# Decoding 64-bit weights: the guard for tiny values as a factor in ScalarE's operation

## The chip, the cores and the metric

The kernel runs on one core of one Trainium2 chip. The metric is the device time of one execution in microseconds (us). A core has five engines that run their own instruction streams in order and wait for one another through semaphores: TensorE (PE in the profile, with its weight loads shown apart as PEld), VectorE (DVE), ScalarE (ACT), GpSimd (POOL) and SyncE (SP), which here issues every DMA. The kernel before was timed in three runs: 1007.31, 1008.38 and 1008.51 us, the median 1008.38 us.

## The reference

Block-causal attention is followed by a gated product of matrices without a nonlinearity. The sizes are batch 8, 8 heads, 576 positions, 64 columns a head; blocks of 64.

```python
scores = scale * np.matmul(q, k.transpose(0, 1, 3, 2))
scores = np.where(block_i >= block_j, scores, -1e9)
attn = np.exp(scores - np.max(scores, axis=-1, keepdims=True))
attn = attn / (np.sum(attn, axis=-1, keepdims=True) + 1e-9)
x = np.matmul(attn, v)                  # laid out as 4608 tokens x 512
a, b = x @ w1, x @ w2                   # w1, w2: 512 x 1024
out = ((a * b @ w3) @ w_out)            # w3: 1024 x 1024, w_out: 1024 x 512
```

The inputs q, k and v are 32-bit floats. The four weight matrices arrive as 64-bit floats, because a 32-bit array was multiplied by a 64-bit scalar.

## The kernel before, in words

Two heads form a pair, and the 32 pairs (8 batches of 4) are worked through one after the other by `pair(n)`. For each pair, `shift_mask` finds row maxima (tiles `mx` on PE, reduced on DVE into `m`, transposed into `mt`, negated by ACT into `ms`, and written by a small DMA into a row of `qk`), `prep_qk` splits q and k into a rounded part and a remainder, `s_tile` makes scores `s` and their exponentials, `pv` or `pv_early` multiplies them with v into `x`, and `norm` and `finish_x` divide by the row sums and split the result into `xh` and `xl` (lines 320 to 333). `gen_moe` then multiplies a batch's four x tiles with w1 and w2 (line 381, tile `ab`) and with the product of w3 and w_out (line 397, tile `o`).

The first four pairs are the early stage. While their attention runs, `gen_w` brings in the weights. It loads 40 pieces of 128 partitions by 512 weights: eight of w_out (tile `wo`), then, in turn, two pieces of w3 (tile `w`) and one of w1 for each of eight steps, and at the end eight of w2. PE multiplies w3 by w_out in the early stage (line 358, 64 matmuls that the trace records as 128), so that only the product `wh`, `wl` is needed later. `load_w`, lines 122 to 143, turns each piece into 32-bit floats. It sees a 64-bit float as two 32-bit words, low and high. One ACT instruction takes the sign off the high word (line 135), one DVE instruction takes the maximum of that with 2 to the power -15 (line 136), one shifts it left by three bits and masks it (line 137), one puts the sign and the top exponent bit back (line 138), and one adds three bits of the low word (line 141). The five buffers `wraw` of the loaded words come free when line 141 has read them. Pieces of w1 and w2 also get a rounded copy by ACT (line 147) and a remainder by DVE (line 148).

The order of instructions on the engines in the early stage is written out in part by `EARLY_PLAN`, a string of steps; in it "C" advances the weight loader. A scheduler with priorities then places each instruction, so an edit in `load_w` can move others. In the main stage PE's order is that of `PLAN`. SP issues its DMAs in one queue, in order: a load that waits for a free buffer holds back those behind it.

Of the kernel before, what the change touches and what calls it, by code (L numbers as in the profile page):

```python
# [7 lines left out]
F32 = mybir.dt.float32  # L8
# [3 lines left out]
AF = mybir.ActivationFunctionType  # L12
ALU = mybir.AluOpType
# [45 lines left out]
def block_causal_attention__then__gated_mlp_kernel(ctx, tc, qkv, consts, ident_in, w1, w2, w3t, wout, out_t):  # L59
    nc = tc.nc  # L60
# [61 lines left out]
    def load_w(dst, src, k):  # L122

        t = tl["early"].tile([P, 1024], F32, tag="wraw", name="wraw", bufs=5)
        u = tl["early"].tile([P, 512], F32, tag="wbits", name="wbits", bufs=6)
        wide = t.bitcast(I32)
        nc.sync.dma_start(out=wide.rearrange("p (k w) -> p k w", k=k), in_=src)  # L130
        wide = wide.rearrange("p (c two) -> p c two", two=2)
        low, high = wide[:, :, 0], wide[:, :, 1]
        bits = u.bitcast(I32)
        V = nc.vector
        nc.scalar.activation(u, high.bitcast(F32), AF.Abs)
        V.tensor_scalar(out=u, in0=u, scalar1=2.0**-15, scalar2=None, op0=ALU.max)
        V.tensor_scalar(out=bits, in0=bits, scalar1=3, scalar2=0x3FFFFFF8, op0=ALU.logical_shift_left, op1=ALU.bitwise_and)
        V.scalar_tensor_tensor(out=bits, in0=high, scalar=-0x40000000, in1=bits, op0=ALU.bitwise_and, op1=ALU.bitwise_or)  # L138
        if dst is None:
            dst = u.unsqueeze(1)  # L140
        V.scalar_tensor_tensor(out=dst.bitcast(I32), in0=low.rearrange("p (k w) -> p k w", k=k), scalar=29,
                               in1=bits.rearrange("p (k w) -> p k w", k=k), op0=ALU.logical_shift_right, op1=ALU.bitwise_or)
        return u

    def load_split(dst_h, dst_l, src):
        val = load_w(None, src.unsqueeze(1), 1)
        nc.scalar.copy(dst_h, val)
        nc.vector.tensor_tensor(out=dst_l, in0=val, in1=dst_h, op=ALU.subtract)
# [187 lines left out]
    def gen_w(wp):  # L336
        wo = tl["wo"]
        for k in range(NF):
            load_w(wo[:, k : k + 1, :], wout[k * P : (k + 1) * P, :].unsqueeze(1), 1)
            yield  # L340
# [8 lines left out]
        for m in range(NF):  # L349
            t3 = wp.tile([P, NF, P], F32, tag="w3", name="w3", bufs=2)  # L350
            for k in range(0, NF, 4):
                src = w3t[k * P : (k + 4) * P, 2 * m * P : 2 * (m + 1) * P].rearrange("(k p) f -> p k f", p=P)
                load_w(t3[:, k : k + 4, :], src, 4)
                if k == 0:
                    yield
            acc = ps_m.tile([P, 512], F32, tag="psm", name=f"w{m}")
            for k in range(NF):
                nc.tensor.matmul(acc, t3[:, k, :], wo[:, k, :], start=(k == 0), stop=(k == NF - 1))  # L358
            pending.append((m, acc))
            if len(pending) > 1:  # L360
                evacuate()
            yield
            next(rows1)
            yield
# [172 lines left out]
```

## Time and profile before

| | |
|---|---|
| Time, median of three runs | 1008.38 us |
| Profiled execution, its own time | 1008.37 us |
| Span in its profile | 1006.6 us (so 1.77 us lie around it) |
| PE busy over the span | 961.6 us, 96% |
| DVE busy over the span | 718.8 us, 71% |
| ACT busy over the span | 547.9 us, 54% |
| Mean granted PE clock | 0.984 |
| DMA | 80.39 MB, mean 80 GB/s |

The shares are means over two very different stages. The early stage, to about 153 us, has DMA rates of some 250 GB/s at first and a full VectorE; in the main stage after it PE is full. A row of the timeline gives the start, the duration, engine, line and shapes, and in brackets how long the engine had been idle and who released it. PE's busy time is modelled, with matmuls overlapping, so a full PE is not one at its peak.

### The profile page before, as it was taken

To read this page: it belongs to the slowest core of one execution; us is meant where nothing else is said; L and a number is where in the kernel's file an instruction comes from. 1 tells how busy PE (TensorE), PEld (TensorE's weight loads), DVE (VectorE), ACT (ScalarE), POOL (GpSimd) and SP (SyncE) were. 2 spreads that over 40 slices of the span, in tenths; PEclk is the share of its full clock that TensorE was granted. 3 is DMA by queue.
4 is the path that set the end of the run, shared out by engine and by line. 5 is a ranking of instruction groups with operands and counts; after the bars stand their busy time and mean duration, and the time that the engine had idled before them with its cause. 6 is when DMAs were issued, how large, how long until landed. Compare 5 with 4: busy or idle time off the path is not lost.

```text
span 1006.6 us, 18165 instructions
## 1 busy us (share of the span) xinstructions
PE 961.6 (96%) x6594; PEld 886.1 (88%) x6624; DVE 718.8 (71%) x1356; ACT 547.9 (54%) x1433; POOL 521.1 (52%) x525
## 2 busy tenths in 40 slices
PE   4699958999999999999999999999999999999998
PEld 2354548999999999999999999999999999999998
DVE  7999997767777777777777767777777777774100
ACT  4655755555565655555555566555555655653211
POOL 0000006667665766666666657576666766573211
PEclk9799978999999999999999999999999999999999
DMA  8776522122212221221222222212212222110000
GB/s 247 240 257 195 170 82 61 55 80 61 85 57 78 61 74 38 70 73 56 78 61 85 61 74 61 84 32 67 73 58 76 61 85 61 37 24 25 1 25 24
DMA packets 36409, 80.39 MB, mean 80 GB/s; under 512 B 4384, under 2 KB 20896, under 8 KB 36320
## 3 DMA queue, kind: packets, MB, share of 16 engines
q1 hardware_dynamic: 36320, 79.23, 26.5%
q8 instruction: 52, 0.85, 0.4%
q14 instruction: 37, 0.30, 0.1%
HBM read 50.76 MB, written 9.44 MB: 60 GB/s over the span
## 4 chain that ended last, share of the span: by engine, by line
PE 60%; DVE 23%; ACT 9%; issue 6%; DMA 2%; DVEq 0%; ACTq 0%
PE ab L381 23%; PE o L397 20%; DVE pl L248 7%; PE s L230 6%; PE x L285 4%; PE mx L179 3%; DVE g L388 2%; ACT ph L246 2%; PE w L358 2%; ACT p L245 2%; DVE m L183 2%; DVE wbits L138 1%; DVE x L323 1%; DVE rb L322 1%; DVE qk L157 1%
## 5 line engine op out<-in xcount | busy, mean ns | idle before, releaser
L251 POOL TENSOR_TENSOR rsum<-rsum,p 128x448 f32<-128x448 f32 x224 | 178.3, 796 | 120.4 <-ACT p L245 113.6
L248 DVE TENSOR_TENSOR pl<-p,ph 128x448 fp32r<-128x448 f32 x168 | 150.9, 911 | 64.1 <-ACT ph L246 63.2
L389 ACT CAST gh<-g 128x288 fp32r<-128x288 f32 x128 | 55.5, 433 | 219.3 <-DVE g L388 219.3
L390 POOL TENSOR_TENSOR gl<-g,gh 128x288 fp32r<-128x288 f32 x128 | 108.3, 846 | 123.0 <-ACT gh L389 122.9
L230 PE MATMUL s<-qk 128*128 128x288 f32 (+4 forms) x768 | 160.7, 317 | 9.2 <-DMA qk<-ms 3.5
L381 PE MATMUL ab<-xh,w1h 128*128 128x288 f32 x512 | 152.0, 297 | 6.8 <-ACT xh L332 6.8
L381 PE MATMUL ab<-xh,w2h 128*128 128x288 f32 x512 | 154.1, 301 | 0.0
L397 PE MATMUL o<-gh,wh 128*128 128x288 f32 x512 | 153.4, 300 | 0.0
L381 PE MATMUL ab<-xh,w1l 128*128 128x288 f32 x512 | 151.6, 296 | 0.0
L381 PE MATMUL ab<-xl,w2h 128*128 128x288 f32 x512 | 151.5, 296 | 0.0
L381 PE MATMUL ab<-xl,w1h 128*128 128x288 f32 x512 | 151.5, 296 | 0.0
L381 PE MATMUL ab<-xh,w2l 128*128 128x288 f32 x512 | 151.4, 296 | 0.0
L397 PE MATMUL o<-gl,wh 128*128 128x288 f32 x512 | 150.8, 295 | 0.0
L397 PE MATMUL o<-gh,wl 128*128 128x288 f32 x512 | 150.8, 295 | 0.0
L207 POOL TENSOR_TENSOR qk<-raw,qk 64x1152 fp32r<-64x1152 f32 x54 | 144.3, 2672 | 2.0
L220 POOL TENSOR_TENSOR vs<-raw,vs 128x320 fp32r<-128x320 f32 x56 | 49.9, 891 | 174.2 <-ACT vs L157 174.2
L230 PEld LDWEIGHTS s<-qk 128*128 128x128 f32 (+1 forms) x768 | 116.9, 184 | 26.1 <-issue 6.1
L183 DVE TENSOR_REDUCE m<-mx 128x1 f32<-128x512 f32 (+6 forms) x320 | 128.6, 449 | 15.8 <-PE mx L179 13.2
L246 ACT ACTIVATE ph<-s 128x288 fp32r<-128x288 f32 x336 | 131.3, 392 | 0.0
L388 DVE TENSOR_TENSOR g<-ab,a 128x288 f32<-128x288 f32 x128 | 57.7, 451 | 74.4 <-PE ab L381 71.2
L245 ACT ACTIVATE p<-s 128x448 f32<-128x448 f32 x224 | 85.5, 382 | 45.8 <-PE s L230 44.2
L285 PE MATMUL x<-ph,vs 128*128 128x128 f32 x336 | 104.1, 319 | 0.0
(71 smaller groups left out, 2141.6 us busy)
## 6 DMA issues: line engine op xcount, KB each, us to landing
raw<-in_qkv SPq DMA_DIRECT2D x32, 896.0 KB
qk<-qk SPq DMA_DIRECT2D x64, 288.0 KB
out_t<-o SPq DMA_DIRECT2D x64, 144.0 KB
wraw<-in_w3t SPq DMA_DIRECT2D x16, 512.0 KB
wraw<-in_w SPq DMA_DIRECT2D x16, 512.0 KB
wraw<-in_wout SPq DMA_DIRECT2D x8, 512.0 KB
qk<-ms SPq DMA_DIRECT2D x64, 2.2 KB
cst<-in_consts SPq DMA_DIRECT2D x1, 288.0 KB
```

What stands on the lines that cost most here:

```text
L183: nc.vector.reduce_max(m[:, col : col + 1], sc, axis=AX.X)
L207: (nc.vector if n <= EARLY else nc.gpsimd).tensor_tensor(out=low, in0=rqk[o], in1=high, op=ALU.subtract)
L230: nc.tensor.matmul(t[ks, at : at + q1 - q0], qk[j][:, 2 + s, kr], qk[j][:, s, q0:q1], start=(s == 0), stop=(s == 1))
L245: nc.scalar.activation(p32, t[ks, at : at + w], AF.Exp, scale=SCALE)
L246: nc.scalar.activation(ph[ks, o : o + w], t[ks, at : at + w], AF.Exp, scale=SCALE)
L248: nc.vector.tensor_tensor(out=low, in0=p32, in1=ph[ks, o : o + w], op=ALU.subtract)
L251: nc.gpsimd.tensor_tensor(out=r, in0=r, in1=p32, op=ALU.add)
L285: nc.tensor.matmul(xps[:, to : to + w], v[:, c, :], pr[:, a : a + w], start=(u < 2 and s == 0), stop=(u in (0, len(PV) - 1) and s == len(p ...
L381: nc.tensor.matmul(t[:, 0:HALF], l[:, c, fs], r, start=(c == 0 and s == 0), stop=(c == NC - 1 and s == 2))
L388: nc.vector.tensor_tensor(out=g32, in0=acc[1][:, 0:HALF], in1=a32, op=ALU.mult)
L390: nc.gpsimd.tensor_tensor(out=gl[:, f, :], in0=g32, in1=gh[:, f, :], op=ALU.subtract)
L397: nc.tensor.matmul(t[:, 0:HALF], l[:, f, es], r[:, f, :], start=(f == 0 and s == 0), stop=(f == NF - 1 and s == 2))
```

## The change

The maximum on VectorE is taken out. ScalarE's operation, which takes the sign off, gets a factor of 2 to the power -112, so its output has an exponent field that is smaller by 112. After the shift by three bits this is the shift of the exponent by 896 that turns a 64-bit exponent into a 32-bit one, and what is too small comes out of ScalarE as a tiny number or zero. The two constants change with it: the mask lets the top exponent bit through, and from the high word only the sign is taken.

```diff
-        nc.scalar.activation(u, high.bitcast(F32), AF.Abs)
-        V.tensor_scalar(out=u, in0=u, scalar1=2.0**-15, scalar2=None, op0=ALU.max)
-        V.tensor_scalar(out=bits, in0=bits, scalar1=3, scalar2=0x3FFFFFF8, op0=ALU.logical_shift_left, op1=ALU.bitwise_and)
-        V.scalar_tensor_tensor(out=bits, in0=high, scalar=-0x40000000, in1=bits, op0=ALU.bitwise_and, op1=ALU.bitwise_or)
+        nc.scalar.activation(u, high.bitcast(F32), AF.Abs, scale=2.0**-112)
+        V.tensor_scalar(out=bits, in0=bits, scalar1=3, scalar2=0x7FFFFFF8, op0=ALU.logical_shift_left, op1=ALU.bitwise_and)
+        V.scalar_tensor_tensor(out=bits, in0=high, scalar=-0x80000000, in1=bits, op0=ALU.bitwise_and, op1=ALU.bitwise_or)
```

The line numbers after the change are one or two higher: shift and mask 138, sign 139, low bits 142, remainder 149, reduction 184, split of k and q 208, product with the reciprocal 324. The main stage's instructions keep their order on every engine. In the early stage the scheduler places them anew. Three places matter.

VectorE ahead of PE's first product of weights; `wo` is w_out's last piece and `w_313`, in the change `w_305`, the first half of the first tile of w3. Before:

```order
L138 SCALAR_TENSOR_TENSOR wbits<-wraw,wbits 128x512
L185 TENSOR_REDUCE m_213<-m_213 128x1
L136 TENSOR_SCALAR wbits<-wbits 128x512
L141 SCALAR_TENSOR_TENSOR wo<-wraw,wbits 128x512
L137 TENSOR_SCALAR wbits<-wbits 128x512
L136 TENSOR_SCALAR wbits<-wbits 128x512
L138 SCALAR_TENSOR_TENSOR wbits<-wraw,wbits 128x512
L137 TENSOR_SCALAR wbits<-wbits 128x512
L141 SCALAR_TENSOR_TENSOR wo<-wraw,wbits 128x512
L138 SCALAR_TENSOR_TENSOR wbits<-wraw,wbits 128x512
L136 TENSOR_SCALAR wbits<-wbits 128x512
L141 SCALAR_TENSOR_TENSOR w_313<-wraw,wbits 128x512
```

And in the change:

```order
L208 TENSOR_TENSOR qk_85<-raw_147,qk_85 64x1152
L184 TENSOR_REDUCE m_208<-mx_5_256 128x1 x2
L142 SCALAR_TENSOR_TENSOR wo<-wraw,wbits 128x512
L186 TENSOR_REDUCE m_208<-m_208 128x1
L138 TENSOR_SCALAR wbits<-wbits 128x512 x2
L139 SCALAR_TENSOR_TENSOR wbits<-wraw,wbits 128x512 x2
L142 SCALAR_TENSOR_TENSOR wo<-wraw,wbits 128x512
L142 SCALAR_TENSOR_TENSOR w_305<-wraw,wbits 128x512
```

The maxima are gone, and the last piece of w_out and the first of w3 now go through each step together, so the shift of w3's first piece stands four instructions ahead of the one that writes `w_305`. From VectorE's first instruction to that point ten instructions are left out and none is added.

VectorE at the end of the early stage, from the transposition of the last early row sums to the product that finishes x of the fourth pair. Before:

```order
L309 STREAM_TRANSPOSE tr_1_1107<-x_1_1034 64x576
L148 TENSOR_TENSOR w2l<-wbits,w2h 128x512
L138 SCALAR_TENSOR_TENSOR wbits<-wraw,wbits 128x512
L310 TENSOR_SCALAR rr_883<-tr_1_1107 64x18
L207 TENSOR_TENSOR qk_85<-raw_864,qk_85 64x1152
L141 SCALAR_TENSOR_TENSOR wbits<-wraw,wbits 128x512
L320 RECIPROCAL rr_883<-rr_883 128x18
L322 STREAM_TRANSPOSE rb_1112<-rr_883 128x576
L148 TENSOR_TENSOR w2l<-wbits,w2h 128x512
L323 TENSOR_TENSOR x_3_882<-x_3_882,rb_1112 128x576
```

And in the change:

```order
L310 STREAM_TRANSPOSE tr_1_1067<-x_1_998 64x576
L149 TENSOR_TENSOR w2l<-wbits,w2h 128x512
L142 SCALAR_TENSOR_TENSOR wbits<-wraw,wbits 128x512
L311 TENSOR_SCALAR rr_853<-tr_1_1067 64x18
L208 TENSOR_TENSOR qk_85<-raw_834,qk_85 64x1152
L149 TENSOR_TENSOR w2l<-wbits,w2h 128x512
L321 RECIPROCAL rr_853<-rr_853 128x18
L323 STREAM_TRANSPOSE rb_1072<-rr_853 128x576
L324 TENSOR_TENSOR x_3_852<-x_3_852,rb_1072 128x576
```

One piece of w2 is further along. Counted from the last remainder `wl` of the weight product (line 347, then 348) to this product, with both ends, the rows before hold four of line 136, four of 137, five of 138, five of 141, six of 148 and three of 207. In the change they hold none of 136, and two, three, four, four and two of the others, and one more 512-wide reduction of `mx`; all else is the same.

SP's queue after the first loads of w3; `raw_353`, in the change `raw_343`, is the q, k and v of the third pair, and `ms` the negated maxima of the second. Before:

```order
L130 DMA wraw<-in_w3t 128x4x256 x2
L130 DMA wraw<-in_w 128x1024
L94 DMA raw_353<-in_qkv 128x1792
L196 DMA qk_84<-ms_272 1x9x64
L130 DMA wraw<-in_w3t 128x4x256 x2
```

And in the change:

```order
L132 DMA wraw<-in_w3t 128x4x256 x2
L132 DMA wraw<-in_w 128x1024
L197 DMA qk_84<-ms_266 1x9x64
L94 DMA raw_343<-in_qkv 128x1792
L132 DMA wraw<-in_w3t 128x4x256 x2
```

The load of the third pair stands behind the small DMA that waits for the second pair's maxima. On PE, the third pair's first two `mx` products now stand right behind the first tile of the weight product and two score products, where before they came behind the second and the third tile.

## The prediction

> **What bounds the kernel now.** I read the slices of the span first, then the busy time by stage, then the waits, then the timelines of VectorE and PE at the places where the stage with the change begins and ends. The slices (40, of 25 us each) and the table by stage (us of the stage, then busy us of PE, PEld, DVE, ACT, POOL, the granted clock, the DMA share and GB/s):
>
> ```profile
> PE   4699958999999999999999999999999999999998
> DVE  7999997767777777777777767777777777774100
> PEclk9799978999999999999999999999999999999999
> ...
> 0.00:50.00 50.00, 27.94 (x86) 15.44 (x87) 42.81 (x87) 26.78 (x50) 1.87 (x7) 0.90 0.80 243
> 50.00:70.00 20.00, 19.85 (x59) 9.90 (x58) 20.00 (x41) 10.46 (x20) 0.00 (x0) 1.00 0.82 268
> 70.00:130.00 60.00, 57.94 (x200) 31.30 (x202) 58.55 (x122) 40.14 (x80) 0.00 (x0) 1.00 0.59 182
> 130.00:152.00 22.00, 11.37 (x44) 7.93 (x44) 20.71 (x41) 10.24 (x21) 1.15 (x1) 0.70 0.25 69
> 152.00:170.00 18.00, 16.50 (x99) 15.70 (x101) 12.45 (x20) 10.14 (x29) 11.26 (x12) 0.80 0.23 69
> ```
>
> DVE's 71% of the span is a mean that hides the case: it is 20.00 of 20 us and 58.55 of 60 in the early stage, the only one in which the removed instruction occurs. PE has holes in the early stage's first 50 and last 22 us and almost none between. In the main stage PE is full, and its longest wait in total there is this row of the waits after 155 us:
>
> ```profile
> PE x L285 <- DVE pl L248: 4.1, 14, 0.3
> ```
>
> So what the main stage takes is set by PE, its order does not move, and the change is worth what it brings forward the main stage's start. That start is seen on three engines:
>
> ```profile
> 126.54 0.68 DVE L347 TENSOR_TENSOR wl<-w,wh 128x512 fp32r<-128x512 f32 x1
> 151.24 1.42 DVE L323 TENSOR_TENSOR x<-x,rb 128x576 f32<-128x576 f32 x1
> 153.02 0.76 ACT L332 CAST xh<-x 128x288 fp32r<-128x288 f32 x2 [1.90 <-DVE x L323]
> 153.50 0.61 PE L381 MATMUL ab<-xh,w1h 128*128 128x288 f32 x1 [6.82 <-ACT xh L332]
> ```
>
> PE stood for 6.82 us before 153.50, for x of the fourth pair, which DVE finished at 152.66 (151.24 and 1.42) after working off the rest of w2.
>
> **What one instruction is worth.** The two groups by line that the edit touches, and five neighbours on DVE's timeline where it never waits, then three more:
>
> ```profile
> L136 DVE TENSOR_SCALAR wbits<-wbits 128x512 f32<-128x512 f32 x40 | 16.5, 417 | 0.3 <-ACT wbits L135 0.3
> L135 ACT ACTIVATE wbits<-wraw 128x512 f32<-128x512 f32 x40 | 26.9, 677 | 19.0 <-DMA wraw<-in_w3t 9.4 <-DMA wraw<-in_w 4.9 <-DMA wraw<-in_wout 2.5
> ...
> 49.74 0.42 DVE L136 TENSOR_SCALAR wbits<-wbits 128x512 f32<-128x512 f32 x1
> 50.08 0.69 DVE L138 SCALAR_TENSOR_TENSOR wbits<-wraw,wbits 128x512 int32<-128x512 int32 x1
> 50.68 0.42 DVE L137 TENSOR_SCALAR wbits<-wbits 128x512 int32<-128x512 int32 x1
> 51.02 0.69 DVE L141 SCALAR_TENSOR_TENSOR w<-wraw,wbits 128x512 int32<-128x512 int32 x1
> 51.62 0.69 DVE L138 SCALAR_TENSOR_TENSOR wbits<-wraw,wbits 128x512 int32<-128x512 int32 x1
> ...
> 64.33 1.34 DVE L207 TENSOR_TENSOR qk<-raw,qk 64x1152 fp32r<-64x1152 f32 x1
> 65.59 0.67 DVE L148 TENSOR_TENSOR w1l<-wbits,w1h 128x512 fp32r<-128x512 f32 x1
> 66.20 0.67 DVE L141 SCALAR_TENSOR_TENSOR w<-wraw,wbits 128x512 int32<-128x512 int32 x1
> ```
>
> Forty maxima of 417 ns make 16.5 us busy, but neighbours overlap: from start to start line 136 takes 0.34 us, 137 also 0.34, 138 and 141 take 0.60, 148 takes 0.61 and 207 takes 1.26. The removal is worth 40 times 0.34, or 13.6 us of DVE's time, not 16.5. The other two DVE edits change constants alone; I cost them at nothing.
>
> ScalarE's factor: no row shows this operation with a factor on weights. The exponentials do multiply, by 0.125 (line 238):
>
> ```profile
> 29.39 0.54 ACT L238 ACTIVATE pe<-s 128x448 f32<-128x448 f32 x1 [0.46 <-PE s L230]
> 120.36 0.41 ACT L238 ACTIVATE pe<-s 128x288 f32<-128x288 f32 x1
> ```
>
> From 288 to 448 columns is 0.13 us, so 512 would take about 0.59 us, below the 0.677 that line 135 takes now. I take nothing. The bounds are minus 0.09 us and, if a factor cost a second pass, plus 0.68 us on each of 40. The latter would add 27 us to ACT, which is busy for 40.14 of 60 us where DVE is full, and would show first where DVE waits for line 135, for 0.3 us in all now.
>
> **The three parts of the early stage.** By the order of VectorE, ten maxima fall before PE's first product of weights, 26 between that and the last remainder `wl`, and four after it.
>
> *Head.* DVE's ten are 3.4 us. What starts PE, and what ACT does before:
>
> ```profile
> 35.38 0.46 ACT L216 COPY ve<-raw 128x320 f32<-128x320 f32 x1 [1.07 <-PE x L269]
> 35.74 1.21 ACT L135 ACTIVATE wbits<-wraw 128x512 f32<-128x512 f32 x2
> ...
> 41.02 0.69 DVE L141 SCALAR_TENSOR_TENSOR w<-wraw,wbits 128x512 int32<-128x512 int32 x1
> ...
> 41.76 9.58 PE L358 MATMUL w<-wo,w 128*128 128x512 f32 x16 [4.41 <-DVE w L141]
> 61.65 7.11 PE L358 MATMUL w<-wo,w 128*128 128x512 f32 x16
> ```
>
> The first w3 piece loses its sign on ACT behind a copy that waits for PE's attention work, so not before about 36.35. In the new order DVE then does one of 138, two of 139 and one of 142 ahead of the one PE waits for: 36.35 and 0.34, 1.20, 0.60 and 0.69 make 39.2, against 41.7. That is 2.5 us if the attention work keeps its times, 3.4 if it does not hold DVE up. I take **2.8**.
>
> *Middle.* DVE loses 26 times 0.34, or 8.8 us. It gains what moves in from the tail: two of 137 (0.7), two of 138 (1.2), one of 141 (0.6), two of 148 (1.2), one of 207 (1.3), less one reduction of `mx` like 141 (0.6), together 4.4. It is 4.4 us shorter. But PE is full as well: 16 matmuls of the weight product in 7.11 us are 0.44 each, 128 of them 57 us, and the attention fills the rest to 57.94 of 60. The gain lies between 0, if PE alone sets the pace, and 4.4, if DVE does. Both are at their limit, so I take half, **2.2**. The loads share the middle at 0.82 and then 0.59 of the DMA engines; they follow the buffers that DVE frees.
>
> *Tail.* From the last `wl` at 126.54 DVE works to 152.66 and is busy for 20.71 of 22 us. It loses four of 136 (1.4), two of 137 (0.7), two of 138 (1.2), one of 141 (0.6), two of 148 (1.2) and one of 207 (1.3), and gains one reduction (0.6): 5.8 us less. DVE's idle 1.3 us there could grow to 3 once attention is waited for more often, so at least 4. I take **5.7**. Next late is PE's own attention for the fourth pair, then the row of maxima for the fifth.
>
> *Clock.* PE's granted clock over stretches of 2 us:
>
> ```profile
> 38.00:40.00 2.00, 0.00 (x0) 0.00 (x0) 2.00 (x5) 0.37 (x2) 0.00 (x0) 0.97 0.22 57
> 40.00:42.00 2.00, 0.24 (x1) 0.24 (x2) 2.00 (x5) 1.76 (x3) 0.00 (x0) 0.50 0.83 263
> 46.00:48.00 2.00, 2.00 (x5) 0.91 (x4) 2.00 (x4) 0.75 (x3) 0.00 (x0) 0.82 0.77 239
> 156.00:158.00 2.00, 2.00 (x10) 2.00 (x10) 1.26 (x2) 1.36 (x4) 1.57 (x2) 0.50 0.57 240
> 158.00:160.00 2.00, 2.00 (x13) 2.00 (x12) 1.50 (x2) 0.37 (x1) 0.69 (x1) 0.66 0.00 0
> ```
>
> After each long hole PE runs at half clock. The first 16 weight matmuls took 9.58 us instead of 7.11, and from 153.50 to some 159.3 the clock was about 0.5, which costs half of 5.8, or 2.9 us, of the stage that PE sets. Shorter holes should cost less at the second place: between 0 and 2.9, I take **1.0**. At the first place I take nothing beside the middle's 2.2.
>
> **Sum.** 2.8 + 2.2 + 5.7 + 1.0 = 11.7 us. The profiled execution took 1008.37 us, 0.01 below the median of the three runs, so **996.7 us**. The least is 2.5 + 0 + 4 + 0 = 6.5, or 1001.9; the most is 3.4 + 4.4 + 5.8 + 2.9 = 16.5, or 991.9.
>
> **The rivals.**
>
> 1. *PE alone binds, and the spare time is lost.* Then the middle gives nothing, and the work moved ahead of the last `wl` makes `wl` late by as much as it shortens the tail: left are 2.5 and the tail's own four maxima, 1.4, so 1004.5. For it speaks PE's 57.94 of 60; against it that DVE's middle gets shorter even with the moved work. Chance 0.12.
>
> 2. *No half clock.* If the holes before the weight product and before the main stage both get short enough, PE keeps its clock: 2.5 us more in the middle, where PE sets the pace, and 1.9 more than my 1.0 at the end, so 11.7 + 4.4 = 16.1 and 992.3. For it speaks that 38 to 40 us still shows 0.97, so that a start some 2 us earlier may come before the fall. Against it, the wait of about 3.5 us for the fifth pair's maxima remains. The Trainium skill, page "TensorE: Matmul & The Clock Gate", part 1 on the HAM clock gate, has half rate after at least one idle window of about 3.4 us and full rate after about as long of sustained work; the rows agree with half rate after the holes of 4.41 and 6.82 us. Chance 0.15.
>
> 3. *The loads bind the head.* 0.80 of the DMA engines are busy in the first 50 us, and line 135 waits for loads for 16.8 us in all. If DVE's earlier requests find no earlier data, the head gives 0 and the middle 0: 5.7 + 1.0 leave 1001.7. Against it: each of those waits was followed by DVE work that was already queued. Chance 0.07.
>
> 4. *Slower: PE is blocked behind the third pair's load.* SP and ACT before:
>
> ```profile
> 32.45 0.43 SPq L94 DMA_DIRECT2D raw<-in_qkv  x1
> 37.68 0.81 SPq L196 DMA_DIRECT2D qk<-ms  x1
> 39.85 0.67 ACT L157 CAST kb<-raw 128x576 bf16<-128x576 f32 x1 [1.63 <-DMA raw<-in_qkv]
> ```
>
> The load took 7.4 us (32.45 to 39.85). It now stands behind the small DMA of 37.68, and PE's queue has that pair's first `mx` right after the first weight tile. Issued at 38.5, it lands near 46, and two casts later, near 48, `mx` can run; PE comes there at 39.2 and 7.1 to 9.6, or 46 to 49. So it costs 0 to 2 us. It decides only if the load lands 12 us later still, which would take back the whole 11.7 and bring another half clock, 2.9: 1011.3. Chance 0.03.
>
> The forecast keeps 0.63. A run tells 0.2%, 2 us, from no change. Only rival 4 is slower; within 0.2% would need nearly all terms to fail together, 0.03; faster is 0.94. The range of 8 in 10 is the sum's own, cut a little at the slow end: 992.0 to 1001.5. It leaves out rivals 1 and 4 and the edges of the others.
>
> **What would show it.** In the new profile DVE has 40 instructions fewer, some 16.5 us less busy time; ACT's group of line 137 keeps 677 ns. PE's first weight matmul starts near 39 instead of 41.76, the last `wl` near 121.5 instead of 126.54, PE resumes with `ab` near 143 instead of 153.50, and from there to the end it takes about 852 us, one less than before (1006.6 less 153.5 is 853.1). I am wrong if line 137 on ACT takes over 0.75 us, if `ab` resumes near 149 with PE full before it (rival 1), or if the main stage itself gets longer.

## The result, and the profile after the change

The changed kernel took **997.65 us** (median of four runs, 996.98 to 999.64). The kernel before, run on the same chip beside it, took 1008.44 us. The ratio is **0.9908, with a 95% interval of 0.9892 to 0.9924**, which is 9.3 us of the 1008.44, with 7.7 to 10.9 as its interval. The two medians lie 10.8 us apart, at the upper end of that; the ratio is not simply theirs. Forecast were 996.7 us and a range of 992.0 to 1001.5.

The profiled execution of the changed kernel is the slowest of its four: 999.64 us, with a span of 997.8. Its span is 8.8 us shorter than the 1006.6 of before. Its rows therefore explain 8.8 us, and the other 2 us of the medians lie in the spread between runs: its mean granted clock is 0.989, that of the other three runs 0.993.

The page of the changed kernel: busy time by engine, then two of the rows that cut the span into 40 slices.

```profile
PE 959.7 (96%) x6624; PEld 884.9 (89%) x6624; DVE 705.7 (71%) x1316; ACT 546.5 (55%) x1433; POOL 520.3 (52%) x525
...
PE   3799979999999999999999999999999999999998
...
PEclk9799989999999999999999999999999999999999
```

DVE has 1316 instructions instead of 1356 and 13.1 us less busy time (705.7 for 718.8). In the first slice PE is at 3 tenths where it was at 4, although DVE's work had become lighter. That is a first hint that the head went another way than forecast.

The stages of the changed kernel, with the columns of the table by stage shown before (stage, its us, busy us of PE, PEld, DVE, ACT, POOL, granted clock, DMA share, GB/s):

```profile
0.00:50.00 50.00, 29.14 (x83) 16.00 (x84) 38.30 (x73) 24.87 (x47) 1.87 (x7) 0.86 0.76 234
50.00:70.00 20.00, 20.00 (x59) 9.71 (x58) 17.60 (x32) 10.05 (x21) 0.00 (x0) 1.00 0.69 229
70.00:130.00 60.00, 57.56 (x202) 31.36 (x201) 58.50 (x116) 41.79 (x84) 0.00 (x0) 1.00 0.68 218
130.00:152.00 22.00, 15.56 (x72) 12.09 (x72) 19.04 (x35) 13.91 (x30) 4.58 (x4) 0.84 0.25 69
152.00:170.00 18.00, 18.00 (x139) 17.52 (x138) 14.07 (x29) 10.81 (x30) 13.67 (x14) 1.00 0.15 34
```

From 50 to 70 us DVE is no longer full (17.60 instead of 20.00 us) while PE has not a hole: 20.00 of 20. From 152 us PE is full at full clock, where before it had 16.50 of 18 us at 0.80.

The points at which the main stage becomes possible, from the changed kernel's timeline (start, duration, engine, line; in brackets the idle time and who ended it):

```profile
126.92 0.69 DVE L348 TENSOR_TENSOR wl<-w,wh 128x512 fp32r<-128x512 f32 x1
...
145.78 0.76 DVE L324 TENSOR_TENSOR x<-x,rb 128x576 f32<-128x576 f32 x1
...
146.63 0.77 ACT L333 CAST xh<-x 128x288 fp32r<-128x288 f32 x2 [1.90 <-DVE x L324]
...
147.11 0.61 PE L382 MATMUL ab<-xh,w1h 128*128 128x288 f32 x1 [3.46 <-ACT xh L333]
```

The last `wl` starts where it started before (126.92 against 126.54). PE resumes with `ab` 6.4 us earlier (147.11 against 153.50). From `ab` to the end it is 850.7 us (997.8 less 147.11) against 853.1. So in this pair of profiles the gain lies behind the last `wl`: 6.4 us before `ab`, and 2.4 after it.

In the main stage nothing else changed. PE's longest wait there, by the waits of the changed kernel from 155 us on, is the same row as before with 4.0 for 4.1:

```profile
PE x L286 <- DVE pl L249: 4.0, 14, 0.3
```

And ScalarE's factor, by the changed kernel's groups by line, is free: 671 ns instead of 677.

```profile
L137 ACT ACTIVATE wbits<-wraw 128x512 f32<-128x512 f32 x40 | 26.2, 671 | 7.8 <-DMA wraw<-in_w 3.7 <-DMA wraw<-in_wout 2.4 <-DMA wraw<-in_w3t 1.3
```

**Why the head gave nothing.** ACT, DVE and PE of the changed kernel ahead of the first weight matmul:

```profile
38.58 0.46 ACT L217 COPY ve<-raw 128x320 f32<-128x320 f32 x1 [4.09 <-PE x L270]
38.95 0.65 ACT L137 ACTIVATE wbits<-wraw 128x512 f32<-128x512 f32 x1
...
39.66 1.24 ACT L137 ACTIVATE wbits<-wraw 128x512 f32<-128x512 f32 x2
...
39.63 0.43 DVE L138 TENSOR_SCALAR wbits<-wbits 128x512 int32<-128x512 int32 x1 [1.78 <-ACT wbits L137]
...
42.52 5.97 PE L359 MATMUL w<-wo,w 128*128 128x512 f32 x7 [3.76 <-DVE w L142]
```

The copy `ve` waits on ACT for PE's second attention product, and the signs of w_out's last piece and of w3's first pieces are queued behind it. Before, it ran at 35.38 after 1.07 us of waiting, and now at 38.58 after 4.09. DVE, ahead of its old schedule, then waits 1.78 us for ACT. From the copy to the first weight matmul are 3.94 us, close to the forecast's 3.8 (35.38 to 39.2). It was the copy that moved. PE had run its attention at half clock until it was nearly done:

```profile
32.00:34.00 2.00, 1.89 (x4) 1.26 (x5) 1.67 (x6) 1.95 (x5) 0.00 (x0) 0.50 1.07 361
34.00:36.00 2.00, 2.00 (x6) 0.77 (x4) 1.19 (x1) 0.49 (x1) 0.00 (x0) 0.50 1.07 399
36.00:38.00 2.00, 2.00 (x8) 1.50 (x6) 1.65 (x5) 0.00 (x0) 0.00 (x0) 0.56 0.06 23
```

(The changed kernel in stretches of 2 us, columns as in the table by stage.)

### The profile page after: what moved, and what is told of

Read it like the earlier page. It is cut to its first block, busy times and chain, and to the rows that moved or that the text cites. A ratio compares the mean times of both kernels' runs of the same rounds, so it can differ in the third digit from the quotient of the medians.

```text
span 997.8 us, 18149 instructions
## 1 busy us (share of the span) xinstructions
PE 959.7 (96%) x6624; PEld 884.9 (89%) x6624; DVE 705.7 (71%) x1316; ACT 546.5 (55%) x1433; POOL 520.3 (52%) x525
## 4 chain that ended last, share of the span: by engine, by line
PE 69%; DVE 17%; ACT 7%; issue 4%; DMA 2%; DVEq 0%; ACTq 0%; SPq 0%
PE ab L382 28%; PE o L398 21%; PE s L231 7%; DVE pl L249 6%; PE x L286 5%; PE mx L180 3%; PE w L359 3%; ACT p L246 2%; DVE g L389 2%; ACT ph L247 2%; PE x L270 2%; DVE m L184 1%; DMA wraw<-in_w 1%; DVE x L324 1%; ACT a L387 1%
```

## The experiments

### Is ScalarE's factor free?

`e1_nofactor` is the change without the factor, with the constants of before. It leaves out the guard for tiny weights altogether. Its instructions stand in the same order on every engine as the changed kernel's.

```diff
-        nc.scalar.activation(u, high.bitcast(F32), AF.Abs, scale=2.0**-112)
+        nc.scalar.activation(u, high.bitcast(F32), AF.Abs)
...
-        ... scalar2=0x7FFFFFF8 ... scalar=-0x80000000
+        ... scalar2=0x3FFFFFF8 ... scalar=-0x40000000
```

> The changed kernel without the factor: ScalarE takes the sign off as before the change, the two constants are those of before, and no guard is left for values below 2 to the power -127 (the kernel leaves out the treatment of tiny weights). VectorE's work and the order on all engines are those of the change. Theory T (the gain is VectorE's removed work at the end of the early stage, the factor is free): within 1 us of 997.6, and ScalarE's sign operation takes 670 to 680 ns as in both traces. Rival F (the factor costs ScalarE something that the trace's mean hides, by waits): 994 to 996.

Measured, as the first theory had it: 998.02 us (997.74 to 998.95), ratio to the kernel before 0.9906 (0.9893 to 0.9919), the changed kernel's 0.9908 within a fraction of its interval. ACT's group of the kernel without the factor:

```profile
L137 ACT ACTIVATE wbits<-wraw 128x512 f32<-128x512 f32 x40 | 26.5, 674 | 9.5 <-DMA wraw<-in_w 5.4 <-DMA wraw<-in_wout 2.2 <-DMA wraw<-in_w3t 1.5
```

It takes 674 ns without the factor, 671 with it. The factor costs nothing, and the bound of plus 0.68 us falls.

Since the order is the same, this run is also a second profile of the change. Its timeline at the points read above:

```profile
36.43 0.46 ACT L217 COPY ve<-raw 128x320 f32<-128x320 f32 x1 [2.52 <-PE x L270]
...
40.37 7.97 PE L359 MATMUL w<-wo,w 128*128 128x512 f32 x14 [3.77 <-DVE w L142]
...
125.34 0.69 DVE L348 TENSOR_TENSOR wl<-w,wh 128x512 fp32r<-128x512 f32 x1
...
145.53 0.61 PE L382 MATMUL ab<-xh,w1h 128*128 128x288 f32 x1 [4.21 <-ACT xh L333]
```

Here the copy runs at 36.43, 2.15 us earlier than in the changed kernel's profile, and the weight product starts 3.94 us later again, at 40.37. The same instructions thus start PE's weight product at 42.52 in one run and 40.37 in another; before it was 41.76. Some 0.6 of the 2.15 us were there before: the first data landed after 5.8 us instead of 6.5. The other 1.5 go with the clock: in 34 to 36 us it was 0.50 in the changed kernel's run and is 1.00 here.

```profile
32.00:34.00 2.00, 2.00 (x5) 1.09 (x4) 1.70 (x4) 1.86 (x3) 0.00 (x0) 0.51 1.08 374
34.00:36.00 2.00, 2.00 (x11) 1.18 (x9) 1.71 (x4) 0.00 (x0) 0.00 (x0) 1.00 0.79 302
```

So the head is anything from 1.4 us won to 0.8 us lost, as far as these two profiles and the one of before show it.

### Where does a maximum cost anything?

Three kernels put a maximum (against zero, which changes no value) back into the changed kernel for some of the pieces: `e2_max_out` for w_out's eight, `e3_max_mid` for the 24 of w3 and w1, `e4_max_w2` for the eight of w2. The line below is added for these pieces alone; the scheduler then orders the early stage anew.

```diff
         nc.scalar.activation(u, high.bitcast(F32), AF.Abs, scale=2.0**-112)
+        if guard:
+            V.tensor_scalar(out=u, in0=u, scalar1=0.0, scalar2=None, op0=ALU.max)
```

> The change, with a maximum with zero, which alters nothing, put back on VectorE for the eight pieces of w_out alone. All eight stand ahead of PE's first product of weights: 8 x 0.34 = 2.7 us more VectorE work in the head. Theory T (the head waits for PE's attention and ScalarE's queue, not for VectorE): 0 to 1 us, so 996.5 to 998.6. Rival S (every maximum was worth the same, 10.8 / 40 = 0.27 us, wherever it stood): 997.6 + 2.2 = 999.8.

> The change, with the maximum put back for the 24 pieces of w3 and w1: two ahead of the first weight product, 22 in the middle, none in the tail. The new order leaves more behind the last wl: two of the shift, one sign, one low-bits, one remainder and one split of k and q more than in the change, by their start-to-start times 0.7 + 0.6 + 0.6 + 0.6 + 1.3 = 3.8 us. Theory T: what counts is what is left behind the last wl, so 3 to 5 us more than the change, 1000.6 to 1002.6, with the last wl within 1 us of the change's 126.9. Rival S: 24 x 0.27 = 6.5 us more, 1004.1. Rival M (PE alone sets the middle and any VectorE work there is free): 997.6.

> The change, with the maximum put back for the eight pieces of w2: none in the head, four in the middle, four behind the last wl. Behind it there are also two shifts and one sign more than in the change: 4 x 0.34 + 0.7 + 0.6 = 2.7 us. Theory T: 2.5 to 3.5 us more, 1000.1 to 1001.1, all of it between the last wl and the product that finishes x of the fourth pair. Rival S: 8 x 0.27 = 2.2 us, 999.8. With the run on w_out's pieces, which has as many maxima, T expects a difference of at least 2 us, S none.

| maxima | median, us | ratio to before | last `wl` starts | `ab` resumes |
|---|---|---|---|---|
| none (the change) | 997.65 | 0.9908 (0.9892 to 0.9924) | 126.92 | 147.11 |
| w_out's 8 | 996.45 | 0.9894 (0.9877 to 0.9912) | 126.40 | 143.74 |
| w3's and w1's 24 | 1003.31 | 0.9955 (0.9939 to 0.9970) | 126.47 | 150.06 |
| w2's 8 | 1001.46 | 0.9932 (0.9918 to 0.9945) | 125.24 | 148.01 |
| all 40 (before) | 1008.44 | 1 | 126.54 | 153.50 |

The time does not go by the number of maxima: eight of w_out and eight of w2 are 5.0 us apart, with intervals that do not overlap, where rival S expected no difference. Eight maxima on w_out's pieces cost nothing that can be measured. The 24 of w3 and w1 do not make the last `wl` later (126.47), as theory T had it; they come due behind it. By their medians all three runs lie just outside theory T's bounds, w_out's 0.05 us below, w2's 0.4 and w3's and w1's 0.7 above; the last is as near to rival S's 1004.1, and it rules out rival M's 997.6. `ab` resumes as follows in the kernel with w_out's maxima:

```profile
143.74 0.61 PE L384 MATMUL ab<-xh,w1h 128*128 128x288 f32 x1 [0.99 <-ACT xh L335]
```

And in the one with the maxima of w3 and w1:

```profile
150.06 0.61 PE L384 MATMUL ab<-xh,w1h 128*128 128x288 f32 x1 [6.12 <-ACT xh L335]
```

With `wl` at the same moment, the stretch from it to `ab` is 17.3 us in the one and 23.6 in the other, 20.2 in the changed kernel and 27.0 before. DVE works off in this stretch what it did not manage ahead of it. The order of the kernel with w_out's maxima happens to leave less of w2 behind `wl`: two signs, three instructions of line 142's kind and three remainders, each one piece less than in the change. By their start-to-start times these are 1.8 of the 2.9 us by which the stretch is shorter; the rest was not taken apart.

### Can other engines take DVE's work?

Four kernels give a piece of DVE's or ACT's work to GpSimd: `e5_ve_pool` the copies `ve` that hold up ACT's queue (those of pairs 1 to 3), `e6_qk4_pool` the fifth pair's split of q and k, `e7_w2l_pool` the remainders of w2, and `e8_all_pool` all three.

```diff
-            nc.scalar.copy(tl["ve", j][:, :, own[j]], rv)
+            (nc.scalar.copy if n == 0 else nc.gpsimd.tensor_copy)(tl["ve", j][:, :, own[j]], rv)
...
-        (nc.vector if n <= EARLY else nc.gpsimd).tensor_tensor(out=low, ...)
+        (nc.vector if n < EARLY else nc.gpsimd).tensor_tensor(out=low, ...)
...
-        nc.vector.tensor_tensor(out=dst_l, in0=val, in1=dst_h, op=ALU.subtract)
+        (nc.gpsimd if low_pool else nc.vector).tensor_tensor(out=dst_l, in0=val, in1=dst_h, op=ALU.subtract)
```

> The change, with the copy of v (line 217) of the second to fourth pair moved from ScalarE to GpSimd, which is idle in the early stage. In the change that copy stood 4.09 us in ScalarE's queue for PE's attention work, and behind it the sign operation of the first pieces of w3, for which VectorE waited 1.78 us. Theory H (the head is held up by this place in ScalarE's queue): the first weight product 2 to 3 us earlier than in the other runs, near 38.5 instead of 40.4 to 42.5, and, PE being full in the middle, the whole 2 to 3 us earlier: 994.6 to 995.6. Rival P (the head waits for PE's half clock and the attention itself, or the middle's end is set by the attention): 997 to 998.

> The change, with the two splits of k and q (line 208) of the fifth pair moved from VectorE to GpSimd; nothing else differs in VectorE's order. Both stand behind the last wl: 2 x 1.26 = 2.5 us less VectorE work there. Theory T: the product that finishes x of the fourth pair comes 2 to 2.5 us earlier after the last wl (17 to 17.6 us instead of 19.6), PE's hole before ab shrinks from 3.5 to about 1 us, 995.0 to 995.6. Rival C (GpSimd's long instructions slow VectorE's beside them, as the one remainder of w2 that took 1.24 us while GpSimd worked): 0 to 1 us gain, 996.6 to 997.6.

> The change, with the eight remainders of w2 (line 149) moved from VectorE to GpSimd. Behind the last wl VectorE has four remainders, two low-bits, two signs and one shift less: 2.4 + 1.2 + 1.2 + 0.3 = 5.1 us by start-to-start times. Theory T: x of the fourth pair up to 5 us earlier after the last wl, but PE's hole is 3.5 us in the change, so 3 to 3.5 us gain, 994.2 to 994.8, and PE's attention sets the start of the main stage. Rival C (VectorE and GpSimd slow each other): VectorE's 512-wide instructions beside GpSimd's above 0.9 us, gain below 1.5 us, over 996.2.

> The change, with all three moves to GpSimd: the copies of v, the fifth pair's splits and the remainders of w2. If head and tail are separate, as T and H hold, the gains add until PE has no hole left before the main stage: 2 to 3 from the head and at most 3.5 and part of the half clock (2) from the tail, 991.5 to 993. If the moves only shift the same wait (rivals P and C): above 994.5.

Measured: 998.20 us (ratio 0.9917, 0.9904 to 0.9929), 998.40 (0.9915, 0.9901 to 0.9929), 1001.38 (0.9944, 0.9931 to 0.9956) and 1002.55 (0.9956, 0.9943 to 0.9970). None beats the change; the last two are slower than it. So all the forecast gains failed (995.6 us or less for the first three, 993 for the last). Even rivals P and C were 0.2 and 0.8 us too low for the first two.

With `ve` on GpSimd the weight product starts at 40.68, after a wait of 2.00 us instead of 3.76:

```profile
38.72 0.27 ACT L190 ACTIVATE ms<-mt 9x128 fp32r<-9x128 f32 x1 [3.87 <-PE mt L188]
...
40.68 7.54 PE L359 MATMUL w<-wo,w 128*128 128x512 f32 x13 [2.00 <-DVE w L142]
```

ACT's queue now stands for the transposed maxima, `mt`, which come out of the same stretch of PE at half clock. That is 1.8 us earlier than in the changed kernel's profile but later than the 40.37 of its twin without the factor, and the median did not move. The queue on ACT explains the place of the wait; it is not worth anything measurable by itself.

The fifth pair's split was to take 2.5 us off DVE in the tail. The tail did not get shorter (19.6 us from `wl` to the finished x, as in the change). GpSimd's and DVE's rows of that kernel say why:

```profile
128.83 3.14 POOL L208 TENSOR_TENSOR qk<-raw,qk 64x1152 fp32r<-64x1152 f32 x1 [126.44 <-ACT qk L158]
...
130.79 1.22 DVE L311 TENSOR_SCALAR rr<-tr 64x18 f32<-64x18 f32 x1
...
133.65 2.61 POOL L208 TENSOR_TENSOR qk<-raw,qk 64x1152 fp32r<-64x1152 f32 x1 [1.67 <-ACT qk L158]
...
134.52 2.29 DVE L139 SCALAR_TENSOR_TENSOR wbits<-wraw,wbits 128x512 int32<-128x512 int32 x1
```

The row sums' `rr` took 1.22 us; in the changed kernel it takes 0.17. It ended at 132.01, just when GpSimd's instruction did (128.83 and 3.14 make 131.97). Line 139, on average 0.68 us, took 2.29 and ended at 136.81, 0.55 us after GpSimd's (136.26). These two stood still beside GpSimd and went on when it was through or soon after. Not every instruction of DVE did: the four reductions of `mx` from 133.39 on, beside the second row of GpSimd, took 1.20 us in all, as in the change (1.22). The Trainium skill, page "SBUF — State Buffer", section "SBUF: two separate sides", describes a port pair that the two engines share as an exclusive lock, held for a whole instruction, with the other one fully blocked; on VectorE's side an instruction with two inputs from SBUF, or in a two-port mode, asks for it. Line 139 has two such inputs, so its row agrees; which condition holds for `rr`, with one input, no run here shows. With the remainders of w2 on GpSimd it is the same:

```profile
116.01 1.51 DVE L138 TENSOR_SCALAR wbits<-wbits 128x512 int32<-128x512 int32 x1
...
129.77 0.68 DVE L348 TENSOR_TENSOR wl<-w,wh 128x512 fp32r<-128x512 f32 x1
...
137.60 1.26 POOL L149 TENSOR_TENSOR w2l<-wbits,w2h 128x512 fp32r<-128x512 f32 x1 [3.22 <-ACT w2h L148]
137.63 1.26 DVE L311 TENSOR_SCALAR rr<-tr 64x18 f32<-64x18 f32 x1
...
143.69 0.28 PE L188 MATMUL mt<-ident,m 128*9 128x128 f32 x1 [0.72 <-DVE m L186]
```

Five of the eight remainders run on GpSimd ahead of the last `wl`, and DVE's instructions beside them take longer, as the shift at 116.01 (1.51 us, usually 0.42). PE is through with the weight product when it is in the change (125.87 against 125.73), but DVE comes to the last `wl` only at 129.77, 2.85 us later than in the change. The loss is made there, by stretched instructions and by a new order of DVE's queue, which no run takes apart: from `wl` to the finished x are 18.6 us, 1.0 less than in the change. The fifth pair's maxima then reached PE only at 143.69 (137.94 in the change), and taking eight instructions of 0.7 us off DVE made the kernel 3.7 us slower than the change.

### What is the half clock worth, and who sets the pace of the middle?

Four kernels keep PE busy in its holes with matmuls whose results nobody reads: `e9_warm_main` ahead of the main stage, `e10_warm_head` ahead of the weight product, `e11_warm_both` at both places, `e12_warm_out` at both places in the kernel with w_out's eight maxima.

```diff
+            for _ in range(6 if m == 0 else 0):
+                nc.tensor.matmul(acc[:, 0:256], wo[:, 6, 0:P], wo[:, 6, 0:256], start=True, stop=True)
             for k in range(NF):
                 nc.tensor.matmul(acc, t3[:, k, :], wo[:, k, :], start=(k == 0), stop=(k == NF - 1))
...
+        for _ in range(14 if (n, j) == (NPAIR, 0) and parts[0][1] == 0 else 0):
+            nc.tensor.matmul(t[:, 0:288], w1h[:, 0, 0:P], w1h[:, 0, 0:288], start=True, stop=True)
...
+                        for _ in range(34 if (b, h, f, c, len(acc)) == (0, 0, 0, NC - 1, 0) else 0):
+                            nc.tensor.matmul(t[:, HALF:512], w1h[:, 0, 0:P], x_of[0, 0, 0][0][:, 0 : 512 - HALF], start=False, stop=False)
```

> The changed kernel, with dummy matmuls on PE in the two holes ahead of the main stage: 14 of 288 columns in the wait for the fifth pair's maxima, 34 of 224 columns (into columns that nobody reads) in the wait for x of the fourth pair. No other engine's order moves. Theory C (the half clock after the holes costs what its rows say): the changed kernel's profile has 0.50 from 147.1 to about 150.2, and the same instructions without the factor have 0.50 from 145.5 to about 149.8. Half of 3.1 to 4.3 us is 1.5 to 2.1 us; the stretch from the resumption of ab to the end shrinks from about 851 to about 849.3, and the median is 995.5 to 996.2. Theory N (PE waits for other engines at the start of the main stage anyway, so a faster clock gives nothing): the granted clock is 1.00 there, the stretch stays at 851 and the median at 997.65.

> The changed kernel, with six dummy matmuls of 256 columns on PE (about 2.7 us) in the wait ahead of the weight product's first tile. The scheduler moves a few instructions of the early stage, among them the third pair's first maxima, one tile of the weight product later. In the changed kernel PE ran at 0.50 from 42.5 to 48, which costs half of 5.5, 2.7 us; without the factor from about 41 to 44.2. Theory C with PE as the bound of the middle: the first 16 weight matmuls take about 7.1 us, the last wl starts some 1.6 to 2.7 us earlier (124.2 to 125.3 instead of 126.9) and the median is 995 to 996. Theory D (DVE sets the pace of the middle): the weight matmuls are faster, but the last wl and the median stay within 0.7 us of the changed kernel's, 997 to 998.3.

> Both sets of dummy matmuls. Theory C: the two gains add up, 993 to 994.5. Theories N and D: 997 to 998.3. If only the one at the main stage's start counts: 995.5 to 996.2.

> The kernel with the maximum back for w_out's eight pieces, the fastest so far at 996.45, with both sets of dummy matmuls (18 instead of 34 ahead of the last group of ab, since the wait there was only 0.99 us). Theory C: its profile has 0.50 from 40.8 to about 44.6 and from 142.5 to about 146.2, half of which is 1.9 and 1.8 us; less what the wait for x keeps, 993 to 994.5. Theories N and D: 996 to 997.

| | median, us | ratio to before | `ab` resumes | from there to the end |
|---|---|---|---|---|
| main stage | 996.09 | 0.9895 (0.9877 to 0.9912) | 146.46 | 849.7 |
| weight product | 995.80 | 0.9886 (0.9867 to 0.9905) | 143.97 | 852.0 |
| both | 994.83 | 0.9881 (0.9861 to 0.9901) | 143.10 | 849.8 |
| both, with w_out's maxima | 994.02 | 0.9872 (0.9854 to 0.9891) | 141.50 | 850.4 |

The kernel before took 1006.11 us beside these four, 2.3 less than beside the change, so the ratios are to be compared and not the medians. By the ratio the first is 1.3 us better than the change, the second 2.2, the third 2.7 and the last 3.6. Only the last one's interval lies clear of the change's, by a hair: **it beats both kernels**. It overlaps that of the same kernel without the dummies (0.9894). Theory C's medians hold for the first, second and last, and the third is 0.3 us above; with the kernel before 2.3 us lower, that says little. What the dummies do is therefore read from the traces.

The main stage's start with the dummies (stretches of 2 us, then PE's resumption) has its full clock:

```profile
146.00:148.00 2.00, 1.49 (x8) 1.22 (x9) 1.36 (x4) 1.25 (x4) 0.00 (x0) 1.00 0.81 301
148.00:150.00 2.00, 2.00 (x17) 2.00 (x17) 1.10 (x1) 1.53 (x4) 1.41 (x2) 1.00 0.31 129
...
146.46 0.40 PE L386 MATMUL ab<-xh,w1h 128*128 128x288 f32 x1 [0.68 <-ACT xh L335]
```

From `ab` to the end it takes 849.7 us, against 850.7 and 851.3 in the two profiles of the change's order and 853.1 before. By these differences the half clock behind the hole was worth 3.4 us before and still is 1.0 to 1.6 in the changed kernel.

The middle, from the first weight matmul to the last `wl`, is one row of the table by stage for each kernel. Before:

```profile
41.76:126.54 84.78, 83.27 (x256) 43.06 (x260) 83.26 (x174) 52.14 (x102) 0.00 (x0) 0.97 0.66 207
```

In the changed kernel, in its twin without the factor, and in the kernel with the fifth pair's split on GpSimd, whose order differs only behind the last `wl`:

```profile
42.52:126.92 84.40, 82.33 (x258) 42.73 (x259) 79.82 (x155) 54.95 (x107) 0.00 (x0) 0.97 0.74 240
...
40.37:125.34 84.97, 83.02 (x258) 42.85 (x259) 79.82 (x154) 55.21 (x107) 0.00 (x0) 0.96 0.73 239
...
41.72:124.85 83.13, 81.56 (x258) 42.30 (x259) 79.64 (x155) 55.04 (x107) 0.00 (x0) 0.98 0.75 245
```

With PE's clock held up ahead of the weight product:

```profile
41.96:124.85 82.89, 81.07 (x258) 41.93 (x261) 80.12 (x156) 54.84 (x107) 0.00 (x0) 1.00 0.73 233
```

DVE's work there fell by 3.4 us (83.26 to 79.82), and the middle by 0.4. Among the three rows of one order DVE's work is the same, and the middle is the longer the lower the clock: 83.13 us at 0.98, 84.40 at 0.97, 84.97 at 0.96. With the clock held up it is another 1.5 us shorter than in the changed kernel (84.40 to 82.89; 2.5 in the kernel with both sets, whose row is 81.92 us long), with nothing taken off DVE. PE's matmuls set the pace of the middle. In rows of 2 us the stretches at 0.50 add up to about 5.0 us of the middle before, and to 5.5, 6.8 and 3.4 in the three rows of the change's order. They cost half of their length: the first 16 weight matmuls took 9.58 us before instead of 7.11, and 9.84 in the changed kernel. Without them the middle would have been, as an estimate, 82.3 us before and 81.4 to 81.7 in the change: DVE's 3.4 us are worth some 0.6 to 0.9 there. The first 16 weight matmuls at full clock:

```profile
41.96 7.13 PE L361 MATMUL w<-wo,w 128*128 128x512 f32 x16 [1.09 <-DVE w L142]
```

They take 7.13 us, so against the changed kernel 2.7 us of clock came out at `wl` as 1.5 to 2.5. A reservation: with the dummies at this place the third pair's first maxima stand a tile later on PE, and its load is issued at 31.98 us again, ahead of the small DMA, and not at 40.63 behind it. So the two causes are not apart to the last microsecond; the three rows of one order do not have this fault.

## Why the prediction was right, and where not

The total was near, 997.65 against 996.7, and inside the range, but two of its four parts were not near. That the sum came so near is in good part luck: a head and a middle that gave little were offset by a tail and a clock that gave more. Two profiles show the change's order, the changed kernel's and its twin's without the factor:

| term | forecast | changed kernel | twin |
|---|---|---|---|
| head, to the first weight matmul | 2.8 | -0.8 | 1.4 |
| middle, from there to the last `wl` | 2.2 | 0.4 | -0.2 |
| tail, from `wl` to `ab` | 5.7 | 6.8 | 6.8 |
| clock, from `ab` to the end | 1.0 | 2.4 | 1.8 |
| sum | 11.7 | 8.8 | 9.8 |

The medians say 10.8, the ratio 9.3. What was missing in the first two rows was made up, in part, by the last two. The last `wl`, forecast near 121.5, started at 126.92 and 125.34, and `ab`, forecast near 143, resumed at 147.11 and 145.53.

**The price of an instruction was right.** 40 times 0.34 makes 13.6 us; DVE's busy time fell by 13.1. The 16.5 that the prediction named as the sign of it in the profile was the wrong figure: the page's busy time counts overlapping neighbours once, so it had to fall by what the sum had used.

**ScalarE's factor at nothing was right**, at 671 against 674 ns.

**The head failed at its condition.** "That is 2.5 us if the attention work keeps its times" was the step, and it does not keep them. The work behind the copy was forecast at 3.8 us and takes 3.94 in both profiles. The copy itself, expected at 35.38, came at 38.58 and 36.43, because PE's attention ahead of it, in a new order, ended later; in the changed kernel's profile half clock until 38 us made it later still. The twin has about as much half clock there as the kernel before, so the 1.05 us by which its copy is later (36.43 against 35.38) are an estimate of what the new order costs; no run takes it apart. The bounds of 2.5 to 3.4 let DVE's queue vary and held that one release fixed.

**The middle failed at "both are at their limit, so I take half".** The truth was near its lower bound, nothing. A stage in which one engine is relieved by 3.4 us and which gets 0.4 shorter, or 0.6 to 0.9 at equal clock, belongs in the main to the other engine. This is the premise of rival 1, to which the prediction gave 0.12, but not its result of 1004.5: the rival added the work that moved in ahead of the last `wl` to the time of `wl`. It cost no time there, because DVE had become slack in the middle. That slack is where the tail's work went for nothing, and it is why the tail kept its whole gain.

**The tail was right in mechanism and 1.1 us short.** DVE between the last `wl` and the finished x, as a row of the table by stage (DVE alone), before:

```profile
126.54:152.66 26.12, 24.76 (x46) 0.74 0.27 79
```

And in the changed kernel, where DVE is the third of the engines:

```profile
126.92:146.54 19.62, 13.39 (x60) 8.94 (x58) 18.75 (x36) 12.27 (x26) 2.37 (x2) 0.91 0.16 33
```

That is 6.0 us less of DVE's work (24.76 less 18.75; forecast 5.8). In addition, the product that finishes x took 1.42 us before and 0.76 now. Before, GpSimd was at work beside it (it ran from 151.24 on):

```profile
150.85 2.52 POOL L220 TENSOR_TENSOR vs<-raw,vs 128x320 fp32r<-128x320 f32 x2 [148.45 <-ACT vs L157]
```

In the change, the same two instructions of GpSimd hit a remainder of w2 instead:

```profile
143.10 2.37 POOL L221 TENSOR_TENSOR vs<-raw,vs 128x320 fp32r<-128x320 f32 x2 [140.71 <-ACT vs L158]
...
143.52 1.24 DVE L149 TENSOR_TENSOR w2l<-wbits,w2h 128x512 fp32r<-128x512 f32 x1
```

That remainder, usually 0.69 us, took 1.24, so most of the loss only changed its place. DVE also waited less (0.9 us of 19.6, before 1.4 of 26.1), where the prediction feared more; and ACT took x up 0.09 us after it was finished instead of 0.36.

**The clock was mis-sized:** 1.0 was taken, 1.8 to 2.4 came, of the 3.4 that were to be had by the kernel with dummies. Rival 2, no half clock, did not occur: both holes remain, 3.76 and 3.46 us, and the rows behind them still show 0.50. Nor is a short hole safe. In the twin the clock fell also at 102 us, though PE had not stood for more than 1.55 us at a time since 92 us:

```profile
102.00:104.00 2.00, 2.00 (x5) 0.87 (x4) 1.99 (x4) 1.96 (x5) 0.00 (x0) 0.56 0.80 258
```

So the length of the hole alone, the condition of this rival, does not decide it here. Of the rival's 4.4 us the kernel with both sets of dummies shows 2.7 by the ratios.

**Rival 3**, loads that bind the head, is not what stopped it: DVE's waits in the changed kernel's first 42 us are for one load, the first of all, and then for ACT and for PE:

```profile
DVE qk L158 <- DMA raw<-in_qkv: 6.5, 1, 6.5
DVE wbits L138 <- ACT wbits L137: 2.2, 2, 1.8
DVE m L184 <- PE mx L180: 1.6, 2, 1.0
```

**Rival 4**, PE blocked behind the third pair's load, did not come: PE runs through from 42.52 on, full from 50 to 70 us. The load was there when ACT cast it at 45.32, the casts were done at 47.25, and PE came to that pair's `mx` only at 52.46, behind its first weight tile. DVE waited once for that pair's maxima, 2.23 us until 52.89, so it was PE that it waited for and not the load.

What is still open is the head's own value in the mean. Two profiles of one order differ by 2.15 us, and only one profile of the kernel before stands against them.

## What to carry to other kernels

When two engines are both full in a stage, work taken off one is worth what the other one leaves it, here 0.4 us of 3.4. But the slack that it makes can be filled with work from behind the stage, and that work is then free. So ask which of it the order lets move forward. And hold no release fixed in a sum because it is not part of the change: name the row that it depends on, and give its movement a bound.

## What was not expected of the hardware

- Some of VectorE's instructions stand still beside GpSimd. One of 0.17 us took 1.22 and one of 0.68 took 2.29, each until GpSimd's own instruction was through or shortly after, while reductions of `mx` kept their time. Work moved from VectorE to GpSimd therefore came back on VectorE (19.6 us of tail with and without it).
- The granted clock differs between runs of the same instructions. PE came back to 1.00 by 34 us in one run and only at 38 in the other, and the first weight matmul moved by 2.15 us, some 1.5 of them with the clock.
- Matmuls that compute nothing kept the clock at 1.00 where they stood, in the waits of 1 to 4 us ahead of the weight product and of the main stage. With them the kernel with w_out's maxima was the fastest, 994.02 us at a ratio of 0.9872; against the same kernel without them, the gain lies within the intervals.
